# One weight block for two batches, a one-instruction gate and a new order of the start in an attention and feed-forward kernel

## The chip, the cores and the metric

The kernel runs on one core of one Trainium2 chip. The metric is the device time of one execution in microseconds (us), the median of several runs on the same chip. The core has TensorE for matmuls (PE in the profile, PEld for its weight loads), VectorE (DVE), ScalarE (ACT), GpSimd (POOL) and SyncE (SP), which here only issues DMAs. Each engine takes its instructions in the order in which they stand in its own queue and waits at an instruction until what it needs is there.

## The reference

Packed attention and two feed-forward networks follow each other. Eight batches of eight heads have 576 tokens with head size 64; 32 packed queries `p` stand between the two attention steps.

```python
p_packed = sm_attn(p, k, v)              # 32 x 64 for each batch and head
out = sm_attn(q, p_packed, p_packed)     # 576 x 64
x = out.transpose(0, 2, 1, 3).reshape(4608, 512)
h = x @ w_in                             # 512 x 2048
x = (h * (1 / (1 + exp(-1.702 * h)))) @ w_out        # 2048 x 512
h = maximum(maximum(x @ w1, x @ w2), x @ w3)         # 512 x 768 each
return h @ w_out2                        # 768 x 512
```

All is float32. `sm_attn` is the softmax attention with scale 1/8.

## The kernel before

**Splitting.** A float32 product is made of three matmuls of a narrower float32 form: each operand is split into a high and a low part (`hi` by a cast on ACT, `lo` by a subtraction on DVE), and `mm3` (L98 to L102) adds low x high, high x low and high x high. So each product shows as three lines, L100, L101 and L102.

**Attention and the first network in one.** A group is one batch and four heads (`Group`, two groups to a batch). Its steps are: load `p` and `k`, scores `s1` (L237), softmax `sm1`, transposes `t1` and `t1r`, product with `v` (`pv`), transpose `pt` to the packed keys; then the scores `s2` of the queries, softmax `sm2` and `sm3`, and a transpose `tr2` to `at`, with its own hi/lo split. The first network does not use the attention's output: since the packed values are only 32 rows per head, `w_in` is multiplied by them first. That product is called `pw`: 128 rows (four heads x 32) by 512 columns of `w_in` for each batch, group and column block n of four. `h = pw x at` then has the depth of the packed rows.

**Two ways to make `pw`.** For batches 0 and 1, `pw1_unit` (L400) works for one batch and one group: the packed values of two pairs of heads stand in a tile `pt` that holds zeros beside them, so that each of two row blocks c of `w_in` takes one `mm3` with 128 columns of which half are zeros; 6 matmuls of 512 columns. For batches 2 to 7, `pw_unit` (L383) works for a pair of batches: a tile `sp` has the packed values of both batches side by side in its 128 columns, 3 matmuls give 64 rows for each of the two batches, and each half is moved out by its own cast on ACT and subtraction on DVE (64x512, L128 and L129). For batches 2 to 7 `w_in` comes back from `wsc`, a copy of the split weights in DRAM.

**Units.** The first network is cut into 256 units of a batch, half of the tokens (288) and 128 columns of `w_in` (`h_unit`, `g_unit`, `out_unit`, L451 to L500). A unit has 6 matmuls into a bank `h`, the gate, and 12 matmuls into the four banks `acc`; the matmuls of unit n are followed by the output matmuls of unit n-2. The gate is x·sigmoid(1.702x), made as 0.5·x·(1 + tanh(0.851x)): a tanh on ACT (L460), a multiplication on DVE (L461), a cast on ACT (L466) and a subtraction on DVE (L468; on POOL for the first two units). The factor 0.5 is put in when the banks `acc` are moved out (L488 to L494). Two banks `h` exist, so unit n+2 waits until the gate of unit n has read its bank.

**Weights.** The eight weight blocks of `w_in` and the eight of `w_out` arrive as 64-bit patterns and are turned into float32 hi/lo on DVE and ACT (`convert`, `convert_low`: L153 to L187). The first four (`wi0`, `wo0`, `wi1`, `wo2`) are loaded and converted beside the first attention groups.

**Second network.** Its weights are converted late in the first network (`Piece`, `conv_late`, L516 to L579, with sums for a product scheme with fewer matmuls), stored, and loaded back in sets; `Set` (L668) and `out2` (L745) do six blocks of 768 tokens. An output tile `o` has three buffers (L754).

**Order.** Nothing runs in the order of the source. `main` (L804) puts each step into a list with a planned time (tables `D_`, `K_`, `L_`, `Q_`, `R_`, `TP_` and numbers in `main`), sorts it, and issues it; a scheduler in the framework then orders each engine's instructions, so a planned time is a wish. `keep_busy` issues matmuls without use between the first attention groups. Eight PSUM banks are in use: two `ph` (for `h`), two `pa` (for scores, transposes and `pw`), and `c0` to `c3` (for `acc`).

## Time and profile before

| What | Value |
|---|---|
| Median of 3 runs (lowest to highest) | 1327.65 us (1327.56 to 1327.84) |
| The profiled execution: its own time | 1326.56 us |
| Its span (first to last instruction) | 1324.70 us, so 1.86 us lie around it |
| Granted TensorE clock | 1.0 of full speed |
| PE busy | 1302.2 us, 98% |
| DVE busy | 914.6 us, 69% |
| ACT busy | 533.5 us, 40% |
| POOL busy | 118.2 us, 9% |
| Matmuls with a moving operand of 512 columns for `pw` | 96 for batches 0 and 1, 144 for batches 2 to 7 |

The stages, by the first matmul of each: the attention of batches 0 and 1 alone until the first unit at 39.5 us, first output matmul at 50.1 us, units until 780.3 us, second network from 780.4 us to the end. A matmul's busy time in the profile overlaps with the next one's, since matmuls are pipelined: the time that one costs is the distance between two starts. PE at 98% is therefore not a measure of its speed; its idle time is what counts, and the idle time is almost all in the first 60 us.

### The profile page before, as it was taken

The numbers are of one execution on the slowest core, as the hardware profiler recorded it, in microseconds if no ns is written. First come the engines' busy times: TensorE is split into PE (matmuls) and PEld (weight loads), VectorE is DVE, ScalarE is ACT, GpSimd is POOL, SyncE is SP. The second block draws the span as 40 slices with busy tenths as digits, with TensorE's granted clock in tenths as the row PEclk, the third lists the DMA queues.
The fourth block names the chain that finished last, engine by engine and source line by source line (L and its number), as shares of the span: only waits on it lengthen the run. The fifth ranks groups of instructions, "written<-read, shape, count | busy, mean of one in ns | idle before, by whom it ended". The sixth has DMA issues, their size and how long they took to land.

```text
span 1324.7 us, 22337 instructions
## 1 busy us (share of the span) xinstructions
PE 1302.2 (98%) x8614; PEld 1224.6 (92%) x8614; DVE 914.6 (69%) x1864; ACT 533.5 (40%) x1140; POOL 118.2 (9%) x250
## 2 busy tenths in 40 slices
PE   6899999999999999999999999999999999999998
PEld 4699888999999989999999999999899899999997
DVE  7999967864656565679999889636556467366461
ACT  4656544653445444556666532311312213123111
POOL 2300001100000000000000011001011011010000
PEclk9999999999999999999999999999999999999999
DMA  9798635624322330336565659847557476475551
GB/s 348 276 385 317 202 107 163 191 86 137 121 68 85 101 125 31 98 111 220 188 210 168 204 186 358 291 158 272 200 202 251 155 268 236 171 251 199 174 176 48
DMA packets 88874, 249.70 MB, mean 188 GB/s; under 512 B 10176, under 2 KB 39360, under 8 KB 81856
## 3 DMA queue, kind: packets, MB, share of 16 engines
q0 software_dynamic: 24640, 132.66, 29.3%
q1 hardware_dynamic: 64128, 115.62, 25.6%
q8 instruction: 68, 1.11, 0.4%
q14 instruction: 38, 0.31, 0.1%
HBM read 204.47 MB, written 43.78 MB: 187 GB/s over the span
## 4 chain that ended last, share of the span: by engine, by line
PE 93%; DVE 4%; DMA 1%; issue 1%; POOL 0%; ACT 0%; SPq 0%; POOLq 0%; ACTq 0%; DVEq 0%
PE acc L100 10%; PE p L102 10%; PE p L100 10%; PE p L101 10%; PE acc L101 10%; PE acc L102 10%; PE h L100 5%; PE h L102 5%; PE h L101 5%; PE accb L102 4%; PE accb L101 4%; PE accb L100 4%; PE pw L100 1%; PE pw L101 1%; PE pw L102 1%; PE pv L287 1%
## 5 line engine op out<-in xcount | busy, mean ns | idle before, releaser
L100 PE MATMUL acc<-g,wo 128*128 128x288 f32 x1024 | 303.7, 299 | 0.0
L102 PE MATMUL acc<-g,wo 128*128 128x288 f32 x1024 | 300.7, 294 | 0.0
L101 PE MATMUL acc<-g,wo 128*128 128x288 f32 x1024 | 300.1, 294 | 0.6 <-POOL g L468 0.5
L100 PEld LDWEIGHTS acc<-g,wo 128*128 128x128 f32 x1024 | 191.7, 188 | 10.4 <-issue 5.3
L101 PEld LDWEIGHTS acc<-g,wo 128*128 128x128 f32 x1024 | 192.5, 188 | 4.7 <-issue 1.0
L102 PEld LDWEIGHTS acc<-g,wo 128*128 128x128 f32 x1024 | 192.3, 188 | 1.6 <-issue 1.5
L460 ACT ACTIVATE t<-h 128x288 f32<-128x288 f32 x256 | 104.9, 411 | 178.5 <-PE h L102 176.6
L461 DVE SCALAR_TENSOR_TENSOR t<-t,h 128x288 f32<-128x288 f32 x256 | 114.7, 450 | 84.1 <-ACT t L460 82.7
L100 PE MATMUL h<-at,pw 128*128 128x288 f32 x512 | 154.9, 303 | 1.4 <-DVE t L461 1.2
L101 PE MATMUL h<-at,pw 128*128 128x288 f32 x512 | 151.6, 296 | 0.4 <-POOL at L125 0.4
L102 PE MATMUL h<-at,pw 128*128 128x288 f32 x512 | 151.1, 295 | 0.0
L466 ACT CAST g<-t 128x288 fp32r<-128x288 f32 x256 | 110.6, 433 | 94.1 <-DVE t L461 92.9
L468 DVE TENSOR_TENSOR g<-t,g 128x288 fp32r<-128x288 f32 x254 | 114.9, 453 | 35.1 <-ACT g L466 34.3
L681 DVE TENSOR_TENSOR u<-s,p 128x384 f32<-128x384 f32 x54 | 29.9, 553 | 119.4 <-PE p L102 119.1
L100 PE MATMUL p<-x_T,ws 128*128 128x384 f32 x324 | 108.3, 334 | 0.0
L101 PE MATMUL p<-x_T,ws 128*128 128x384 f32 x324 | 108.3, 334 | 0.0
L102 PE MATMUL p<-x_T,ws 128*128 128x384 f32 x324 | 108.2, 334 | 0.0
L100 PEld LDWEIGHTS h<-at,pw 128*128 128x128 f32 x512 | 96.1, 188 | 9.8 <-issue 5.6
L101 PEld LDWEIGHTS h<-at,pw 128*128 128x128 f32 x512 | 96.4, 188 | 1.8 <-POOL at L125 1.3
L102 PEld LDWEIGHTS h<-at,pw 128*128 128x128 f32 x512 | 96.2, 188 | 0.1
L711 ACT COPY s<-p 128x384 f32<-128x384 f32 x54 | 25.9, 479 | 161.9 <-PE p L102 161.7
L129 DVE TENSOR_TENSOR pw<-pw,pw 64x512 fp32r<-64x512 f32 (+1 forms) x110 | 74.9, 686 | 18.6 <-ACT pw L128 17.6
(175 smaller groups left out, 2632.0 us busy)
## 6 DMA issues: line engine op xcount, KB each, us to landing
ws<-wss POOLq DMA_DIRECT2D x54, 1024.0 KB, 7.5
wa<-wsa POOLq DMA_DIRECT2D x54, 768.0 KB, 4.6
wi<-wsc POOLq DMA_DIRECT2D x48, 512.0 KB, 3.9
k<-in_k SPq DMA_DIRECT2D x16, 576.0 KB, 4.5
q<-in_q SPq DMA_DIRECT2D x16, 576.0 KB, 4.3
x2d<-x SPq DMA_DIRECT2D x16, 576.0 KB, 4.0
wss<-ws SPq DMA_DIRECT2D x36, 256.0 KB, 4.0
xr<-x2d SPq DMA_DIRECT2D x24, 384.0 KB, 4.3
```

What stands on the lines that cost most here:

```text
L100: nc.tensor.matmul(o, al, bh, start=start, stop=False, skip_group_check=more)
L101: nc.tensor.matmul(o, ah, bl, start=False, stop=False, skip_group_check=more)
L102: nc.tensor.matmul(o, ah, bh, start=False, stop=stop, skip_group_check=more)
L129: nc.vector.tensor_tensor(out=lo, in0=o, in1=f(hi), op=ALU.subtract)
L287: self.mm = nc.tensor.matmul(o[x * D:x * D + D, :P], self.et[:, c * P + x * D:c * P + x * D + D], self.v[:, c, y * P:y * P + P], start=c = ...
L460: nc.scalar.activation(t, o, AF.Tanh, scale=0.5 * 1.702)
L461: nc.vector.scalar_tensor_tensor(out=t, in0=t, scalar=1.0, in1=o, op0=ALU.add, op1=ALU.mult)
L466: latest["act"] = nc.scalar.copy(g[:, 0], gt[n])
L468: latest["dve"] = eng.tensor_tensor(out=g[:, 1], in0=gt[n], in1=f(g[:, 0]), op=ALU.subtract)
L681: latest["dve"] = nc.vector.tensor_tensor(out=o, in0=a, in1=b, op=op)
L711: latest["act"] = nc.scalar.copy(self.s1, self.b1)
```

## The change

Five things are done, all inside the first network and the start, but for the buffers at the end.

- **Pairs.** For column blocks 1 to 3 of batches 0 and 1, `pw_unit` with pair 0 takes the place of four `pw1_unit` calls each. For that each packed tile `pt` of batches 0 and 1 is also copied into a pair tile `sp`, four POOL copies of 128x64 per group (new L344), which stand in POOL's queue among the copies for the next groups. Block 0 stays as it was.
- **Gate.** Units 8 to 28, 114 to 131 and 189 to 255 (106 units) use one ACT instruction for x·sigmoid(1.702x) instead of tanh and a DVE multiplication; their low part is a plain subtraction. The other 150 units keep tanh and multiplication, and now multiply by 0.5 in the cast and in the subtraction; moving out `acc` no longer multiplies, and for batches 0 and 1 all four `acc` banks are moved out by ACT where a running sum does not exist yet (before: two by ACT, two by DVE). The low parts of units 0 and 1 move from POOL to DVE. The one-instruction gate is in another activation table than the exponential; the built program has 7 more table loads on ACT: at units 8, 114, 116 and 189 for the gate, and ahead of the exponentials of group (2,0), of batch 5 group 1 between units 115 and 116, and of batch 6 group 0 after unit 134.
- **Banks.** The first three groups take their first scores from the banks `ph` and their `pv` and `ptp` from `c0`, which no unit uses yet, instead of from the two `pa` banks.
- **Buffers.** The late weights have 3 raw buffers instead of 2; in the second network a temporary `t` has 3 instead of 4 and the output tile `o` has 2 instead of 3.
- **Plan.** All planned times are new. `k` of group (0,1) is now loaded after `v` and `q` of group (0,0), after `wo0` and after `wi1`; before it was loaded right after `wi0`.

```diff
-D_ = [-2, -8, 2.9, -2.51, 2.83, -0.47, -3.58, -0.6, 0.92, -0.32, -6.66, 0.91, 2.97, 2.32, -5.59, -0.32]
+D_ = [[-4.99, -8, 5.53, ...], [2.8, -9.03, 4.99, ...]]
...
+G_ = [8, 29, 114, 132, 189]
+PAIR0 = 1
...
-    def pa_tile(name):
+    def pa_tile(name, early=None):
+        if early in ("h0", "h1"):
+            return ps_h.tile([P, TB], F32, tag="ph", name=name)
+        if early:
+            return ps_c.tile([P, TB], F32, tag=early, name=name)
         return ps_a.tile([P, TB], F32, tag="pa", name=name)
...
+    EARLY = {"s1_0": "h0", "s1_1": "h1", "pv": "c0", "ptp": "c0"}
...
+            if self.b < 2 and PAIR0 < 4:
+                for x in range(2):
+                    for c in range(2):
+                        d = (c ^ self.b) * P + c * D
+                        nc.gpsimd.tensor_copy(sps[key][x][:, d:d + D], f(to[x][:, c * 192:c * 192 + D]))
...
+    def direct(n):
+        return G_[0] <= n < G_[1] or G_[2] <= n < G_[3] or n >= G_[4]
...
-        nc.scalar.activation(t, o, AF.Tanh, scale=0.5 * 1.702)
-        nc.vector.scalar_tensor_tensor(out=t, in0=t, scalar=1.0, in1=o, op0=ALU.add, op1=ALU.mult)
+        if direct(n):
+            latest["act"] = nc.scalar.activation(t, o, AF.Gelu_apprx_sigmoid)
+        else:
+            nc.scalar.activation(t, o, AF.Tanh, scale=0.5 * 1.702)
+            nc.vector.scalar_tensor_tensor(out=t, in0=t, scalar=1.0, in1=o, op0=ALU.add, op1=ALU.mult)
...
-            elif dc % 2 == 0:
-                nc.scalar.mul(x2[:, dc], o, 0.5)
+            elif dc % 2 == 0 or b < 2:
+                nc.scalar.copy(x2[:, dc], o)
...
-            self.raw = late["r"].tile([P, 2 * TB], I32, tag="raw", bufs=2, name=f"wraw_{self.n}")
+            self.raw = late["r"].tile([P, 2 * TB], I32, tag="raw", bufs=3, name=f"wraw_{self.n}")
...
-            t = late["f"].tile([P, DM], F32, tag="o", bufs=3, name=f"o_{j}_{tt}")
+            t = late["f"].tile([P, DM], F32, tag="o", bufs=2, name=f"o_{j}_{tt}")
...
-                for b in range(2):
-                    add(max(t + .1, tn[start[b, n]] - PL_[b], tpt[b, g]), pw1_unit, b, g, n)
+                for x in range(2):
+                    if n < PAIR0:
+                        add(max(t + .1, tn[start[x, n]] - PL_[x], tpt[x, g]), pw1_unit, x, g, n)
+                    else:
+                        add(max(t + .1, tn[start[0, n]] - 10 + 2 * x, tpt[1, g]), pw_unit, 0, 2 * g + x, n)
```

On PE, at column block 3 of batch 0, the kernel before has these twelve matmuls (`wi0_3` and `wi1_3` are the block's weights for groups 0 and 1, `pt_0_0` the packed tile of batch 0, group 0):

```order
L100 MATMUL pw_0_0_3_1809<-wi0_3_1584,pt_0_0_339 128x512
L101 MATMUL pw_0_0_3_1809<-wi0_3_1584,pt_0_0_339 128x512
L102 MATMUL pw_0_0_3_1809<-wi0_3_1584,pt_0_0_339 128x512
L100 MATMUL pw_0_0_3_1809<-wi0_3_1584,pt_0_0_339 128x512
L101 MATMUL pw_0_0_3_1809<-wi0_3_1584,pt_0_0_339 128x512
L102 MATMUL pw_0_0_3_1809<-wi0_3_1584,pt_0_0_339 128x512
L100 MATMUL pw_0_1_3_1818<-wi1_3_1513,pt_0_1_405 128x512
L101 MATMUL pw_0_1_3_1818<-wi1_3_1513,pt_0_1_405 128x512
L102 MATMUL pw_0_1_3_1818<-wi1_3_1513,pt_0_1_405 128x512
L100 MATMUL pw_0_1_3_1818<-wi1_3_1513,pt_0_1_405 128x512
L101 MATMUL pw_0_1_3_1818<-wi1_3_1513,pt_0_1_405 128x512
L102 MATMUL pw_0_1_3_1818<-wi1_3_1513,pt_0_1_405 128x512
```

In the changed kernel the same place on PE has these six, with the pair tiles `sp` (its lines L114 to L116 are `mm3`):

```order
L114 MATMUL pw_0_0_3_1816<-wi0_3_1518,sp_0_263 128x512
L115 MATMUL pw_0_0_3_1816<-wi0_3_1518,sp_0_263 128x512
L116 MATMUL pw_0_0_3_1816<-wi0_3_1518,sp_0_263 128x512
L114 MATMUL pw_0_2_3_1824<-wi1_3_1430,sp_1_426 128x512
L115 MATMUL pw_0_2_3_1824<-wi1_3_1430,sp_1_426 128x512
L116 MATMUL pw_0_2_3_1824<-wi1_3_1430,sp_1_426 128x512
```

Six more, for the other two row blocks, follow 22 rows later, and with them the block is done for both batches; before, twelve more stand some 300 rows later for batch 1. In each of blocks 1 to 3, 24 matmuls become 12.

On DVE, the end of the softmax of group (0,1) stands before like this, from the maximum's subtraction `a` to the transpose into `at_0_1` (`tmp_wo2`, `raw_wo2` and `wo2` are a weight block's conversion, `pn_1_0` and `pt_1_0` belong to the next batch):

```order
L346 TENSOR_REDUCE st2_0_1_482<-a_0_1_476 128x18
L178 SCALAR_TENSOR_TENSOR tmp_wo2_519<-raw_wo2_249,tmp_wo2_519 128x1024
L180 SCALAR_TENSOR_TENSOR tmp_wo2_519<-raw_wo2_249,tmp_wo2_519 128x1024
L347 TENSOR_SCALAR st2_0_1_482<-st2_0_1_482 128x18
L184 TENSOR_SCALAR raw_wo2_249<-tmp_wo2_519 128x1024
L348 RECIPROCAL st2_0_1_482<-st2_0_1_482 128x18
L185 SCALAR_TENSOR_TENSOR wo2_520<-tmp_wo2_519,raw_wo2_249 128x2x512
L292 SCALAR_TENSOR_TENSOR pn_1_0_540<-pv_1_0_529,st1_1_0_427,mask_87 128x128
L349 TENSOR_TENSOR a_0_1_476<-a_0_1_476,st2_0_1_482 128x576
L129 TENSOR_TENSOR pt_1_0_559<-ptp_1_0_556,pt_1_0_559 128x2x64
L356 STREAM_TRANSPOSE at_0_1_580<-a_0_1_476 128x576
```

In the changed kernel it is this on DVE (its L382 is the transpose, L198 and L199 are the old L184 and L185, L143 is L129):

```order
L194 SCALAR_TENSOR_TENSOR tmp_wo2_590<-raw_wo2_355,tmp_wo2_590 128x1024
L374 RECIPROCAL st2_0_1_492<-st2_0_1_492 128x18
L192 SCALAR_TENSOR_TENSOR tmp_wo2_590<-raw_wo2_355,tmp_wo2_590 128x1024
L375 TENSOR_TENSOR a_0_1_486<-a_0_1_486,st2_0_1_492 128x576
L309 SCALAR_TENSOR_TENSOR pn_1_0_540<-pv_1_0_529,st1_1_0_447,mask_87 128x128
L382 STREAM_TRANSPOSE at_0_1_584<-a_0_1_486 128x576
L198 TENSOR_SCALAR raw_wo2_355<-tmp_wo2_590 128x1024
L143 TENSOR_TENSOR pt_1_0_555<-ptp_1_0_552,pt_1_0_555 128x2x64
L199 SCALAR_TENSOR_TENSOR wo2_591<-tmp_wo2_590,raw_wo2_355 128x2x512
```

The last two conversion steps of `wo2` and the low part of `pt_1_0` now stand behind the transpose into `at_0_1` instead of ahead of it.

## Rows read from the trace of the kernel before

**Rows 1.** Five stretches: us, then busy us of PE, PEld, DVE, ACT, POOL
```profile
core 0: us, PE busy (x) PEld busy (x) DVE busy (x) ACT busy (x) POOL busy (x), PEclk, DMA share, GB/s
5.00:35.00 30.00, 18.74 (x221) 13.46 (x222) 26.12 (x49) 12.88 (x28) 6.78 (x16) 1.00 1.03 383
60.00:200.00 140.00, 139.60 (x1006) 128.17 (x1005) 121.06 (x237) 79.60 (x163) 9.45 (x20) 1.00 0.69 256
80.00:160.00 80.00, 79.89 (x569) 73.81 (x568) 73.94 (x142) 48.29 (x92) 4.51 (x11) 1.00 0.80 298
600.00:760.00 160.00, 158.59 (x1172) 156.01 (x1171) 153.12 (x370) 93.68 (x208) 2.66 (x5) 1.00 0.59 195
760.00:1324.70 564.70, 561.13 (x3071) 535.06 (x3069) 334.49 (x616) 135.13 (x245) 56.16 (x106) 1.00 0.61 211
```

**Rows 2.** Chain that ended last, 30 to 80 us: start us, us, what
```profile
44.38 0.70 DVE at L356
...
45.91 1.40 POOL at L125
50.01 0.81 POOL g L468
...
74.58 2.39 DVE wi L163
```

**Rows 3.** Timeline of PE from 178 us: start us, us, instruction
```profile
178.02 0.40 PE L100 MATMUL pw<-wi,pt 128*128 128x512 f32 x1
...
180.59 0.40 PE L102 MATMUL pw<-wi,pt 128*128 128x512 f32 x1
180.82 0.30 PE L100 MATMUL acc<-g,wo 128*128 128x288 f32 x1
```

**Rows 4.** Groups by line and shape: busy us, mean ns, idle us before
```profile
L461 DVE SCALAR_TENSOR_TENSOR t<-t,h 128x288 f32<-128x288 f32 x256 | 114.7, 450 | 84.1 <-ACT t L460 82.7
L460 ACT ACTIVATE t<-h 128x288 f32<-128x288 f32 x256 | 104.9, 411 | 178.5 <-PE h L102 176.6 <-ACT e L259 0.3 <-ACT g L466 0.2
L129 DVE TENSOR_TENSOR pw<-pw,pw 64x512 fp32r<-64x512 f32 x96 | 65.6, 686 | 17.5 <-ACT pw L128 16.7
L494 DVE TENSOR_SCALAR x<-acc 128x288 f32<-128x288 f32 x32 | 13.6, 449 | 0.0
L220 POOL COPY pbd<-praw 64x64 f32<-64x64 f32 x32 | 10.4, 324 | 17.5 <-DMA praw<-in_p 16.1
L129 DVE TENSOR_TENSOR pw<-pw,pw 128x512 fp32r<-128x512 f32 x14 | 9.2, 683 | 1.0 <-ACT pw L128 0.9
L112 ACT ACT_TABLE_LOAD x1 | 1.3, 1283 | 0.7 <-PEq L996 0.7
```

**Rows 5.** Timeline of DVE, 40 to 45 us
```profile
40.99 0.69 DVE L184 TENSOR_SCALAR raw_wo<-tmp_wo 128x1024 int32<-128x1024 int32 x1
...
41.77 1.17 DVE L185 SCALAR_TENSOR_TENSOR wo<-tmp_wo,raw_wo 128x1024 fp32r<-128x1024 f32 x1
...
44.09 0.29 DVE L129 TENSOR_TENSOR pt<-ptp,pt 128x128 fp32r<-128x128 f32 x1 [0.22 <-ACT pt L128]
44.30 0.77 DVE L356 STREAM_TRANSPOSE at<-a 128x576 f32<-128x576 f32 x1
```

**Rows 6.** Timeline of PE, 13 us: the first scores of group (0,1)
```profile
13.18 1.19 PE L242 MATMUL s<-k,pbd 128*64 128x288 f32 x8 [2.74 <-POOL pbd L220]
```

**Rows 7.** Waits: who waited for whom, us in total, times, longest
```profile
PE h L100 <- DVE t L461: 1.2, 2, 0.9
```

**Rows 8.** Timeline of ACT, second network: first and third of three output tiles
```profile
855.88 0.59 ACT L755 COPY o<-accb 128x512 f32<-128x512 f32 x1 [0.74 <-PE accb L102]
...
858.60 0.59 ACT L755 COPY o<-accb 128x512 f32<-128x512 f32 x1 [0.77 <-PE accb L102]
```

**Rows 9.** DMA issues: times, KB each, median us to landing
```profile
out<-o SPq DMA_DIRECT2D x36, 256.0 KB, 2.0
```

More of the change, by code (lines that the diff above doesn't have):

```diff
@@ L31 @@
 SCALE = 1.0 / D ** 0.5
-D_ = [-2, -8, 2.9, -2.51, 2.83, -0.47, -3.58, -0.6, 0.92, -0.32, -6.66, 0.91, 2.97, 2.32, -5.59, -0.32]
-W_ = [60, 15.02, 42.09, 0]
-K_ = [2, 11, -8, 6, 1, -7, 10, 6, -11, -14, -9, -5, -2, -13, -1, 4]
-L_ = [8.18, 16.49, 4, 22.39]
+W_ = [64.48, 18.42, 56.79, 0]
+K_ = [2.01, 11, -10.89, 8.67, 7.12, -5.04, 5.65, 6.8, -16.14, -14.99, -7.49, 1.03, -5.37, -19.64, 5.48, 3.47]
+L_ = [9.04, 16.23, 0.89, 19.91]
 Z_ = [1, 1, 1, 0, 0, 0, 0, 0, 0, 0, 0, 0, 0, 0, 0, 0]
-PL_ = [10, 12]
-Q_ = [12, 9, 9, 8]
-R_ = [32, 23, 17, 5]
-TP_ = [6.0, 8.5, 5.0]
+PL_ = [10.25, 12.07]
+Q_ = [10, 4, 12, 5]
+R_ = [31, 25, 19, 13]
+TP_ = [6.97, 9.09, 5.28]
+D_ = [[-4.99, -8, 5.53, 5.12, 10.41, -1.7, -4.78, -0.6, -1.23, -3.15, -14.11, -6.79, 3.67, 4.23, 0.62, 2.56], [2.8, -9.03, 4.99, -1.86, -6.98, -0.47, -3.58, -0.31, -6.65, -0.14, -0.97, -0.25, 2.63, 0.24, -9.41, -1.18]]
+A_ = [-1.26, 8.77, 21.07, 33.84]
+AS_ = [0.78, 1.07, 0.91, 0.94]
+T_ = [40.71, 1.23, 1.16, 10]
+B2_ = [70.77, 18, 1.2, 5.18]
+B4_ = [20, 10.7, 1.2, 38]
+PC_ = [-11.47, 6.42, 5.47, 8.52, 9, 15.08, 10.31, 11.78]
+G_ = [8, 29, 114, 132, 189]
+X_ = [252, 2.6]
+PAIR0 = 1
 @with_exitstack
@@ L207, in __init__ @@
             self.swap = b & 1 if b >= 2 else 0
+            self.early = EARLY if 2 * b + g < 3 else {}
         def load_pk(self):
@@ L304, in pt @@
                 to = ptt[self.b, self.g] = [t[:, HALF * x:HALF * x + 2 * P] for x in range(2)]
+                key = 0, self.g
+                if key not in sps and PAIR0 < 4:
+                    t = u_tile(f"sp_{self.g}", F32R)
+                    sps[key] = [t[:, HALF * x:HALF * x + 2 * P] for x in range(2)]
             else:
@@ L465, in g_unit @@
         g = gp.tile([P, 2, HALF], F32R, tag="g", name=f"g_{n}")
-        latest["act"] = nc.scalar.copy(g[:, 0], gt[n])
-        eng = nc.gpsimd if n < 2 else nc.vector
-        latest["dve"] = eng.tensor_tensor(out=g[:, 1], in0=gt[n], in1=f(g[:, 0]), op=ALU.subtract)
+        if direct(n):
+            latest["act"] = nc.scalar.copy(g[:, 0], gt[n])
+            latest["dve"] = nc.vector.tensor_tensor(out=g[:, 1], in0=gt[n], in1=f(g[:, 0]), op=ALU.subtract)
+        else:
+            latest["act"] = nc.scalar.mul(g[:, 0], gt[n], 0.5)
+            latest["dve"] = nc.vector.scalar_tensor_tensor(
+                out=g[:, 1], in0=gt[n], scalar=0.5, in1=f(g[:, 0]), op0=ALU.mult, op1=ALU.subtract
+            )
         gt[n] = g
@@ L580, in load_wo2 @@
     def load_wo2(fc):
-        raw = late["r"].tile([P, 2 * TB], I32, tag="raw", bufs=2, name=f"wraw_o{fc}")
+        raw = late["r"].tile([P, 2 * TB], I32, tag="raw", bufs=3, name=f"wraw_o{fc}")
         nc.sync.dma_start(raw, w_out2[fc])
@@ L797, in attention @@
             after = {9: 7, 13: 12, 12: 11, 11: 10, 10: 8, 8: 6, 6: 5, 5: 3, 3: 1, 4: 2, 1: 0}.get(k)
-            tk = t + dt * stretch + (D_[k] if b == 0 else 0) + (dq if k in (7, 9, 11, 12, 13) else 0)
+            tk = t + dt * stretch + (D_[g][k] if b == 0 else 0) + (dq if k in (7, 9, 11, 12, 13) else 0)
             ts.append(tk if after is None else max(tk, ts[after] + .05))
```

43 lines of the change are left out of this document (21 added, 22 removed).

## The prediction

> **What bounds the kernel now.** I read the stretches first [rows 1]. From 60 us to the end PE is idle for 0.4 us of 140, 1.4 of the 160 late ones and 3.6 of the last 565, while DVE is busy 86% from 60 to 200 us and 96% from 600 to 760. So after 60 us whatever is taken off PE shortens the kernel, as long as DVE can follow. The reader is to see there that the two numbers belong to different questions: PE sets the pace, DVE is the engine that would set it next. The first 60 us are another stage: the chain of waits [rows 2] runs through DVE until the transpose that makes `at` of group (0,1), then ACT and POOL split it, and only then can the first unit be finished; its gate's low part on POOL (0.81 us) is the last thing before output matmuls flow. The chain comes back to DVE at 74.58 us, where a conversion of `w_in` is waited for. So the start is a DVE queue, and what stands in it ahead of that transpose counts.
>
> **The change part by part.**
>
> *Pairs.* A batch's block was 2 groups of 6 matmuls, so 24 for the two batches, and is 12 now, since one 128-column operand carries both batches without zeros. Three blocks: 36 matmuls fewer. Twelve of them stand on PE between 178.02 and 180.82 us [rows 3], that is 0.233 us from start to start (the 0.40 us of a row overlaps the next). 36 x 0.233 = 8.4 us. They stood after 60 us, beside other PE work, and all of PE's work there is on the path: -8.4 us.
>
> The price is on DVE: a block's eight results are moved out as halves of 64 partitions, which take as long as whole ones (686 against 683 ns [rows 4]). Three blocks had 12 subtractions and have 24: 12 x 0.686 = +8.2 us. Taken away in the same stretch are the gate multiplications of 21 units (8 to 28), 21 x 0.450 = 9.5 us, and 8 moves of `acc` that ACT now does, 8 x 0.449 = 3.6 us. Together DVE loses 4.8 of 121.1 us in the stretch in which PE loses 8.4 of 140. Its share would go from 86% to 88%. Tightest is 80 to 160 us, where DVE was busy 73.9 of 80 us [rows 1] and most of the new subtractions fall: there PE loses only about 3 us and DVE may gain one. I take +0.5 us of new PE waits; bounds -0.4 (what PE lost there before) and +4.
>
> *Start.* The old L184, L185 and L129 no longer stand ahead of the transpose for (0,1): from start to next start 0.6, 1.1 and 0.2 us [rows 5], 1.9 us off the DVE chain. What is late next is POOL: in its queue two copies into the pair tile for the next batch now stand ahead of the low part of `at`; the nearest row is a POOL copy of 64x64 at 324 ns [rows 4], the new ones are 128x64; 2 x 0.32 = 0.6 us if they are not hidden by the wait for ACT. The low part of the first unit's gate moves from POOL to DVE, where a maximum, a subtraction and two reductions of other groups stand between; I count that at nothing. Sum -1.3, say -1.4 with a little for the waits that vanish. Bounds: DVE was idle 3.9 of the 30 us from 5 to 35 [rows 1], so at best 1.9 + 3.9 = -5.8; at worst all eight new copies for the first two groups delay it, 2.6 - 1.9 = +0.7.
>
> *Early banks.* They only lift waits for `pa`; the units need `ph` and `c0` after 39 us, when these uses are over. Nothing by itself; its worth is inside the start.
>
> *Gate.* Of 1.2 us that PE waited for the multiplication at two units [rows 7], both after 600 us, and 1.4 us that it was idle there in all, the units from 189 on remove the cause: 67 x 0.450 = 30 of DVE's 153 us in that stretch. I take -1.3; bounds 0 and -1.4. The new instruction is not in the trace; the tanh takes 411 ns for the same bank [rows 4]. Were it twice that, the gate would still be shorter than tanh plus multiplication, 861 ns. The other 150 units have the same number of instructions; multiplying in the cast and subtraction is free by shape.
>
> *Table loads.* Seven, each 1283 ns [rows 4], 9.0 us of ACT. ACT waits 176.6 us for `h` over the 256 units, 0.69 us for each, and a load needs no operand, so it runs in that wait and is late by about 0.6 us; the unit after the next, which needs the bank, then has the multiplication's 0.45 us in hand and twelve output matmuls besides. I take +0.5 in all; bounds 0 and 9.0.
> The Trainium skill, "ScalarE: Activation LUTs", says in its section "Rules for kernel authors" to budget about 2.7 us for every switch to a different set. The row above shows 1.28 for the load and an ACTIVATE right after it, so the trace does not bear out more for the load itself; by the page the seven would be 18.9 us of ACT, an estimate that only matters if none of it is hidden.
>
> *Buffers.* With two `o` tiles the third copy in a row, 2.7 us after the first [rows 8], waits for the first's store, which lands 2.0 us after its issue in the median [rows 9]; issue follows the copy (0.6 us), so it is late by nothing at the median. Behind it on ACT stand only further output copies, and PE needs that bank one round of output tiles later. 0 for this, and 0 for `t`, which only DVE writes and reads. The third raw buffer lets loads run ahead: 0.
>
> Sum: -8.4 - 1.4 - 1.3 + 0.5 + 0.5 = -10.1 us. Against the profiled execution's own 1326.56 us that is 1316.5; the median of the runs shown is 1.1 us above it, so 1317.5 us.
>
> **Rivals.**
>
> 1. *DVE takes over from 80 to 160 us.* For it: 92% busy, halves that cost as much as wholes, conversions in the same queue. Against it: half of the removed matmuls or more stood later, where DVE has room. Half of PE's gain given back, +4.2: 1321.7 us.
>
> 2. *The start gets later.* `k` of group (0,1) now stands behind 3.3 MB more (`v`, `q`, `wo0`, `wi1`) at 383 GB/s [rows 1], an estimate of 8.6 us; the scores started at 13.18 us, and POOL was what they waited for [rows 6]. For it: DVE's chain for (0,1) begins with them. Against: DVE has a weight conversion and the softmax of (0,0) to do meanwhile. If half of the delay shows, +4.3 in place of -1.4: 1323.2 us.
>
> 3. *Table switches stop PE; slower.* If the load does not run ahead but in the gate's line, each costs PE the load and the restart of one gate, 1.28 + 0.41 + 0.45 = 2.1 us; seven are 15.0 in place of 0.5: 1332.0 us. It decides from 1.5 us each, where the rest of the gain is used up; the trace's ACT, idle half of the time, speaks against it. The skill's rule quoted above would have it so, with 18.9 us.
>
> 4. *The new order also removes what PE still loses.* All idle time after 60 us up to 760 gone (2.8 us) and the best start: 1317.5 - 4.4 - 2.5 = about 1310.6 us.
>
> **How the numbers follow.** Forecast 0.66, rival 1 0.13, rival 2 0.08, rival 3 0.05, rival 4 0.08. A run of this kernel can tell about 0.2% (2.7 us) from no change: faster means below 1325.0, slower above 1330.3. Forecast, rivals 1 and 4 and nearly all of 2 are faster: 0.91. Rival 3 at its full price is slower, 0.04; what lies between is 0.05. The range: low end at rival 4, 1310.5; high end just above rival 2, 1324.0. Forecast alone: 1314 to 1321.
>
> **What would show it.** Right: 36 fewer 512-column matmuls for `pw`; PE still idle under 1 us from 60 to 200; the first output matmul about 1.4 us earlier than 50.1; the second network's first matmul about 10 us earlier than 780.4; its length unchanged. Wrong: PE rows from 80 to 160 that wait for DVE or for a conversion (rival 1); scores of (0,1) that wait for `k`, and a first output matmul after 50.1 (rival 2); PE waits just behind a table load, or a gate instruction well over 0.86 us (rival 3); a second network that is longer than before (a buffer after all).

## The result, and the profile after

The changed kernel takes 1315.38 us in the median of four runs (1313.53 to 1315.88); the kernel before took 1327.74 us in four runs beside it. The ratio is 0.9901, with a 95% interval from 0.9884 to 0.9918. The forecast was 1317.5 us, range 1310.5 to 1324.0. The profiled execution took 1315.11 us, its span is 1313.0 us (before 1324.7): 11.7 us less.

To see where they went, the span is cut at events that both kernels have: the first output matmul, and the first matmul of units 16, 48 and 184 in the timeline of PE. The 18 matmuls of a unit are the same in both, so a stretch is shorter by the matmuls that left it or by waits that ended. Times in us:

| Stretch | before | changed | difference |
|---|---|---|---|
| start to first output matmul | 50.1 | 50.9 | +0.8 |
| to unit 16 | 43.5 | 44.1 | +0.6 |
| units 16 to 48 (60 matmuls of `pw`, then 24) | 104.4 | 97.2 | -7.2 |
| units 48 to 184 (123 of `pw` in both) | 399.6 | 397.3 | -2.3 |
| unit 184 to the end | 727.1 | 723.5 | -3.6 |
| span | 1324.7 | 1313.0 | -11.7 |

The second network alone took 544.2 us in both. All 36 matmuls left units 16 to 48; 36 x 0.233 = 8.4 us were taken out and 1.2 of them came back. PE's idle time shows only 0.25 us of that: it was 0.11 us in this stretch before and is 0.36 now.

The stretches of [rows 1], read in the changed kernel:

```profile
core 0: us, PE busy (x) PEld busy (x) DVE busy (x) ACT busy (x) POOL busy (x), PEclk, DMA share, GB/s
5.00:35.00 30.00, 20.39 (x218) 14.34 (x218) 25.38 (x46) 12.62 (x27) 8.43 (x15) 0.89 0.96 349
60.00:200.00 140.00, 138.71 (x1014) 127.30 (x1013) 124.37 (x232) 92.39 (x190) 11.06 (x22) 1.00 0.70 257
80.00:160.00 80.00, 79.64 (x568) 73.52 (x567) 75.93 (x132) 59.70 (x115) 4.51 (x11) 1.00 0.79 297
600.00:760.00 160.00, 160.00 (x1202) 159.17 (x1201) 137.54 (x315) 97.05 (x211) 2.53 (x4) 1.00 0.56 188
```

From 600 to 760 us PE is never idle now (the waits of [rows 7] have no row any more), and VectorE has 137.5 us of work there in place of 153.1. From 80 to 160 us VectorE is fuller than before (75.9 of 80, before 73.9) and PE still hardly waits. The first row has the surprise: a granted clock of 0.89 near the start, where before it was 1.00.

The groups that answer to [rows 4]; the columns are those of before:

```profile
L143 DVE TENSOR_TENSOR pw<-pw,pw 64x512 fp32r<-64x512 f32 x120 | 81.9, 687 | 21.1 <-ACT pw L142 19.5
L490 ACT ACTIVATE t<-h 128x288 f32<-128x288 f32 x106 | 43.5, 411 | 59.9 <-PE h L116 59.1
L490 ACT ACT_TABLE_LOAD x4 | 5.1, 1283 | 2.7 <-PE h L116 2.7
L344 POOL CAST sp<-pt 128x64 fp32r<-128x64 f32 x16 | 10.1, 664 | 1.3 <-ACT pt L142 1.2
```

The one-instruction gate takes 411 ns like the tanh. The third row says that ScalarE's idle time ahead of the four loads (2.7 us) was ended by `h`: these loads did not run while ScalarE waited for `h`; they started when `h` was there and stand between `h` and the gate. On ScalarE, at units 8 and 9:

```profile
76.32 1.28 ACT L490 ACT_TABLE_LOAD   x1 [2.44 <-PE h L116]
77.62 0.71 ACT L490 ACTIVATE t<-h 128x288 f32<-128x288 f32 x2
```

PE has no idle time in the 6 us behind any of the seven added loads all the same. A copy into a pair tile takes 664 ns in the mean; I had priced it at 324.

What stood at the place of [rows 6], PE before the first scores of group (0,1), and POOL in the same time:

```profile
14.37 1.19 PE L351 MATMUL s<-q,ptf 128*64 128x288 f32 x8 [0.35 <-ACT ptf L338]
21.38 2.19 PE L259 MATMUL s<-k,pbd 128*64 128x288 f32 x8 [5.83 <-POOL pbd L237]
...
17.93 0.76 POOL L237 COPY pbd<-praw 64x64 f32<-64x64 f32 x1 [4.31 <-DMA praw<-in_p]
18.63 2.40 POOL L344 CAST sp<-pt 128x64 fp32r<-128x64 f32 x2
21.10 0.23 POOL L237 COPY pbd<-praw 64x64 f32<-64x64 f32 x1
```

The scores came 8.2 us later than before. `praw` landed at 17.8 us (before 11.7), and then two pair copies, 2.40 us, stood between the two halves of `pbd`. PE was idle for 5.8 us.

At the end of the start, [rows 2] had the low part of `at` of (0,1) on POOL at 45.91 and the gate's low part on POOL at 50.01. Now, on POOL and then on VectorE:

```profile
45.13 1.48 POOL L344 CAST sp<-pt 128x64 fp32r<-128x64 f32 x2 [1.23 <-ACT pt L142]
46.57 1.39 POOL L139 TENSOR_TENSOR at<-at,at 128x576 fp32r<-128x576 f32 x1
...
49.03 0.46 DVE L493 SCALAR_TENSOR_TENSOR t<-t,h 128x288 f32<-128x288 f32 x1 [1.77 <-ACT t L492]
...
51.46 0.45 DVE L503 SCALAR_TENSOR_TENSOR g<-t,g 128x288 fp32r<-128x288 f32 x1
```

Two more pair copies end just before the low part of `at`, and the gate's low part waits behind four instructions of other groups, left out here. Neither is what made the start late. The low part of `at` ends 2.40 us after ScalarE's cast; in the kernel of "Late copies" below, where no copy stands ahead of it, it takes 2.27 us instead of 1.39 and ends 2.42 us after the cast (before: 1.54). And for the gate's low part PE waits 0.37 us, where it waited 0.45 before.

What is late is the first unit: its first matmul starts at 41.4 us (before 39.5), and from there to the first output matmul it is 9.5 us (before 10.6). PE waits ahead of it for zeros that POOL writes into a tile `pt`:

```profile
38.95 0.50 PE L114 MATMUL pw<-wi,pt 128*128 128x512 f32 x1 [1.80 <-POOL pt L320]
```

```profile
35.70 1.12 POOL L237 COPY pbd<-praw 64x64 f32<-64x64 f32 x2 [3.49 <-DMA praw<-in_p]
36.90 1.74 POOL L139 TENSOR_TENSOR at<-at,at 128x576 fp32r<-128x576 f32 x1
38.60 0.30 POOL L320 MEMSET pt<- 128x256 f32 x1
```

The zeros stand in POOL's queue behind the low part of `at` of (0,0), and that behind a copy of a `praw` that landed at 35.6 us (in the kernel before, the one at this place landed at 32.1).

### The profile page after: what moved, and what is told of

Its sections match the earlier page's. It is cut to its first block, busy times and chain, and to the rows that moved or that the text cites. A ratio compares the mean times of both kernels' runs of the same rounds, so it can differ in the third digit from the quotient of the medians.

```text
span 1313.0 us, 22139 instructions
## 1 busy us (share of the span) xinstructions
PE 1292.8 (98%) x8578; PEld 1219.2 (93%) x8578; DVE 884.3 (67%) x1764; ACT 552.6 (42%) x1167; POOL 128.4 (10%) x264
## 4 chain that ended last, share of the span: by engine, by line
PE 93%; DMA 2%; DVE 2%; POOL 1%; issue 1%; ACT 1%; SPq 0%; POOLq 0%; DVEq 0%; ACTq 0%
PE acc L114 10%; PE p L116 10%; PE p L115 10%; PE p L114 10%; PE acc L115 10%; PE acc L116 10%; PE h L114 5%; PE h L116 5%; PE h L115 5%; PE accb L115 4%; PE accb L116 4%; PE accb L114 4%; PE pv L304 1%; PE s L351 1%; PE s L259 1%; DMA praw<-in_p 1%
## 5 line engine op out<-in xcount | busy, mean ns | idle before, releaser
L114 PE MATMUL acc<-g,wo 128*128 128x288 f32 x1024 | 304.9, 299 | 0.2 <-DVE x L525 0.2
L116 PE MATMUL acc<-g,wo 128*128 128x288 f32 x1024 | 300.6, 294 | 0.0
L114 PEld LDWEIGHTS acc<-g,wo 128*128 128x128 f32 x1024 | 191.8, 188 | 9.2 <-issue 5.1
L116 PEld LDWEIGHTS acc<-g,wo 128*128 128x128 f32 x1024 | 192.3, 188 | 1.0 <-issue 0.9
L114 PE MATMUL h<-at,pw 128*128 128x288 f32 x512 | 154.3, 301 | 0.0
L116 PE MATMUL h<-at,pw 128*128 128x288 f32 x512 | 151.7, 296 | 0.0
L493 DVE SCALAR_TENSOR_TENSOR t<-t,h 128x288 f32<-128x288 f32 x150 | 67.5, 451 | 74.2 <-ACT t L492 73.5
L492 ACT ACTIVATE t<-h 128x288 f32<-128x288 f32 x150 | 61.7, 411 | 122.4 <-PE h L116 121.3
L114 PE MATMUL p<-x_T,ws 128*128 128x384 f32 x324 | 108.3, 334 | 0.0
L116 PE MATMUL p<-x_T,ws 128*128 128x384 f32 x324 | 108.1, 334 | 0.0
L114 PEld LDWEIGHTS h<-at,pw 128*128 128x128 f32 x512 | 96.3, 188 | 7.8 <-issue 6.5
L143 DVE TENSOR_TENSOR pw<-pw,pw 64x512 fp32r<-64x512 f32 (+1 forms) x122 | 83.2, 686 | 21.1 <-ACT pw L142 19.5
L116 PEld LDWEIGHTS h<-at,pw 128*128 128x128 f32 x512 | 96.2, 188 | 1.3 <-issue 1.3
L502 ACT ACTIVATE g<-t 128x288 fp32r<-128x288 f32 x150 | 66.7, 446 | 50.0 <-DVE t L493 49.5
L503 DVE SCALAR_TENSOR_TENSOR g<-t,g 128x288 fp32r<-128x288 f32 x150 | 69.1, 461 | 25.5 <-ACT g L502 25.0
```

What stands on the lines that cost most here:

```text
L114: nc.tensor.matmul(o, al, bh, start=start, stop=False, skip_group_check=more)
L116: nc.tensor.matmul(o, ah, bh, start=False, stop=stop, skip_group_check=more)
L143: nc.vector.tensor_tensor(out=lo, in0=o, in1=f(hi), op=ALU.subtract)
L492: nc.scalar.activation(t, o, AF.Tanh, scale=0.5 * 1.702)
L493: nc.vector.scalar_tensor_tensor(out=t, in0=t, scalar=1.0, in1=o, op0=ALU.add, op1=ALU.mult)
L502: latest["act"] = nc.scalar.mul(g[:, 0], gt[n], 0.5)
```

## The experiments

All stretches are in us, as in the table above; "median" is of all runs of a kernel, the stretches are of the profiled one. The kernel before ran beside each group, on several chips, and took 1326.9 to 1328.2 us in the median, so a difference of about 1 us between kernels of different groups tells nothing.

| Kernel | to first output | to 16 | 16 to 48 | 48 to 184 | 184 to end | median |
|---|---|---|---|---|---|---|
| before | 50.1 | 43.5 | 104.4 | 399.6 | 727.1 | 1327.7 |
| changed | 50.9 | 44.1 | 97.2 | 397.3 | 723.5 | 1315.4 |
| changed, again | 50.7 | 44.0 | 97.2 | 397.3 | 723.3 | 1315.0 |
| no pairs | 48.0 | 43.9 | 103.9 | 397.3 | 723.8 | 1318.7 |
| before with pairs | 50.9 | 44.5 | 110.2 | 398.9 | 726.0 | 1333.9 |
| no gate | 49.9 | 44.0 | 102.9 | 397.3 | 724.3 | 1322.5 |
| all gates | 50.0 | 45.3 | 97.6 | 397.8 | 733.8 | 1326.3 |
| old plan | 53.7 | 44.4 | 102.1 | 398.9 | 727.8 | 1329.6 |
| old buffers | 51.5 | 44.0 | 97.2 | 397.3 | 732.6 | 1323.8 |
| late copies | 49.0 | 44.0 | 97.1 | 397.3 | 723.7 | 1313.6 |
| late copies, again | 47.6 | 44.0 | 97.1 | 397.3 | 724.1 | 1313.2 |
| late copies, POOL gate | 50.8 | 45.0 | 97.1 | 397.3 | 723.6 | 1314.8 |
| late copies, early `k` | 55.1 | 44.0 | 97.1 | 397.3 | 724.3 | 1319.6 |
| late copies, PE filled | 51.4 | 44.0 | 97.1 | 397.3 | 723.6 | 1315.3 |

### No pairs

```diff
-PAIR0 = 1
+PAIR0 = 4
```

> The changed kernel with the old way of blocks 1 to 3 (six matmuls for each batch and group, 36 more of 512 columns in all) and without the 16 copies into the pair tiles; all else, the plan too, stays. Theory (the pairs are worth their matmuls, 36 x 0.233 = 8.4 us, and the copies on GpSimd cost the start about 1 us): 1315.4 + 8.4 - 1 = 1322.8 us, 1321.5 to 1324. First rival (VectorE gave part of it back through the 24 half-size subtractions): less than that returns, 1318 to 1321. Second rival (most of the gain came from the new plan and the gate, the pairs are hidden): under 1318 us.

Measured: 1318.71 us, ratio to before 0.9931 (0.9919 to 0.9944). Only 3.3 us more than the changed kernel: the first rival's range, at its low end. But the stretches give another reason than the rival's. Units 16 to 48 are 6.7 us longer, so little of the 8.4 us was given back there; the first output matmul comes 2.9 us earlier without the pair copies.

### Before with pairs

```diff
+                    if n < 1:
                         add(max(t + .1, ...), pw1_unit, b, g, n)
+                    else:
+                        add(max(t + .1, tn[start[0, n]] - 10 + 2 * b, tpt[1, g]), pw_unit, 0, 2 * g + b, n)
```

with the pair tiles and the four copies of `pt` (L318 to L344 of the changed kernel).

> The kernel before with the pairs alone (pair tiles, their 16 GpSimd copies, 36 matmuls fewer); old gate, plan, banks and buffers. Theory (PE bounds everything after 60 us, the copies cost the start about 1 us): 1327.7 - 8.4 + 1 = 1320.3 us, 1319 to 1321.5. Rival (without the shorter gate in 80 to 160 us VectorE, busy 92% there, has 8.2 us more to do and PE waits for it): 1322 to 1326 us, with PE waits for VectorE between 80 and 200 us.

Measured: 1333.90 us, ratio 1.0048 (1.0035 to 1.0060): slower than before, and slower than either side expected. PE's waits from 95 to 206 us, as "who waited for whom: us in total, times, longest" (the kernel before has no row in that stretch):

```profile
PE ptp L298 <- DVE pn L292: 2.3, 1, 2.3
PE acc L100 <- DVE x L497: 1.5, 2, 1.4
PE pw L100 <- DVE pw L129: 1.5, 1, 1.5
PE h L100 <- DVE t L470: 1.2, 1, 1.2
...
PE acc L101 <- DVE g L477: 0.7, 1, 0.7
```

Most are waits for VectorE. With the longest of them, which ends at 160.97 us, the granted clock also fell to half (PEclk is the third number from the end):

```profile
159.90:166.70 6.80, 5.73 (x19) 3.83 (x20) 3.72 (x10) 1.30 (x4) 0.00 (x0) 0.50 0.21 76
```

It is the same 36 matmuls, and units 16 to 48 are 5.8 us longer than before instead of 8.4 shorter: 14.2 us lost, of which PE's idle time shows 9.0.

### No gate

```diff
-G_ = [8, 29, 114, 132, 189]
+G_ = [999, 999, 999, 999, 999]
```

> The changed kernel with tanh and multiplication in all 256 units: 106 x 0.45 = 48 us more on VectorE, and no table loads but the first. Theory (the short gate takes away PE's waits in acc and h after 200 us, most of them after 600 us): 1.5 to 3 us longer, 1317 to 1318.5 us, with the waits back at 600 to 650 us. First rival (it is what lets VectorE keep up with the pairs at 80 to 160 us): 4 us or more, above 1319.4 us, with waits there. Second rival (the table loads cost about as much as the shorter gate gives): 1314 to 1316 us.

Measured: 1322.47 us, ratio 0.9956 (0.9942 to 0.9969), the first rival. The profiled run was the shortest of the five (1320.5). Units 16 to 48 are 5.7 us longer than in the changed kernel, the stretch after unit 184 only 0.8. PE's longest waits in this kernel from 93 to 197 us, then the only one of the changed kernel from 95 to 192 us:

```profile
PE h L114 <- DVE t L493: 1.4, 1, 1.4
PE pw L114 <- DVE pw L143: 1.0, 1, 1.0
PE acc L114 <- DVE x L525: 0.9, 2, 0.6
...
```

```profile
PE acc L114 <- DVE x L525: 0.2, 1, 0.2
```

The 106 gate units were mostly worth it at the 21 units beside the pairs, not at the 67 late ones.

### Old plan

All 14 tables of planned times hold the values of before, two of them shown; pairs, gate, banks and buffers stay:

```diff
-A_ = [-1.26, 8.77, 21.07, 33.84]
+A_ = [0.0, 8, 20, 34]
...
-PC_ = [-11.47, 6.42, 5.47, 8.52, 9, 15.08, 10.31, 11.78]
+PC_ = [-8, 4, 5, 6.5, 9, 0, 10, 10.5]
```

> The changed kernel (pairs, gate, banks, buffers) with all planned times as before. The pairs alone made the old kernel 6 us slower, and without the gate the changed kernel is 7 us slower. Theory (pairs need both: the gate takes work from VectorE, and the new plan spreads what is left): the gate repairs about half of the loss, 1324 to 1329 us, with PE waits for VectorE left between 95 and 205 us. Rival (the gate alone makes room for the pairs, the plan only orders the start): 1315 to 1319 us. A time above 1331 would mean that the gate's place, units 8 to 28, does not meet the waits of the old plan.

Measured: 1329.60 us, ratio 1.0010 (1.0000 to 1.0020). All of the gain is gone, a little beyond the theory's range. It goes in every stretch: 2.8 us at the start, 4.9 in units 16 to 48, 1.6 in 48 to 184, 4.3 after.

With these four kernels, the stretch of units 16 to 48 can be set side by side. Without waits, 104.4 - 8.4 = 96.0 us would be left:

| | old plan | new plan |
|---|---|---|
| pairs, tanh only | 110.2 (14.2 lost) | 102.9 (6.9 lost) |
| pairs, short gate | 102.1 (6.1 lost) | 97.2 (1.2 lost) |
| no pairs | 104.4 (tanh) | 103.9 (short gate) |

The gate gives 8.1 us with the old plan and 5.7 with the new one, the plan 7.3 or 4.9. (The left column's tanh kernel also has the old banks and buffers, and moves `acc` out on both engines.) PE's idle time in the stretch is 9.0, 4.2, 3.4 and 0.4 us in the four kernels with pairs, in the order of the table's rows, and the granted clock in it 0.97, 1.00, 0.98 and 1.00, so with the old plan a part of the loss is slow matmuls behind the waits. The plan's part is one of order and not of work: with the old plan VectorE is busy for 86.4 us of the stretch, in the changed kernel for 87.7, without the gate for 93.5.

### All gates

```diff
-G_ = [8, 29, 114, 132, 189]
+G_ = [0, 999, 999, 999, 999]
```

> The changed kernel with the one-instruction gate in all 256 units, so between the exponentials too: 50 table loads on ScalarE in place of 8, 42 more, 150 x 0.45 = 68 us less on VectorE. Theory (a load runs while ScalarE would wait for h, and PE does not see it): loads cost PE under 0.1 us each, VectorE's relief gives back up to 3 us of the waits that PE has at 95 to 192 us: 1312 to 1318 us. Rival (each switch stands in the gate's line and costs PE 2.1 us, as worked out in the third rival of the prediction): 42 x 2.1 = 88 us, 1403 us; at 1.28 us each, the load alone, 1369 us. In between, the excess over 1315.4 divided by 42 is the price of a switch.

Measured: 1326.29 us, ratio 0.9988 (0.9979 to 0.9997). That is 10.9 us above the changed kernel, far from 88. All 42 added loads stand before 582 us, and from the first output to unit 184 it took 540.7 us in place of 538.6: 2.1 / 42 = 0.05 us per load, with VectorE's relief already set against it. So PE hardly sees them, and the third rival falls by its price. Its condition, the load in the gate's line, holds: all 25 loads ahead of a gate start after the last `h` matmul of their unit. What hides them must then be the room behind the gate, until unit n+2 needs the bank; that was not tested by itself. The Trainium skill, "ScalarE: Activation LUTs", section "Rules for kernel authors", budgets about 2.7 us per switch, by which 42 would be an estimated 113 us; the run does not bear that out for PE.

Most of the loss stands where no load is, 10.3 us after unit 184, 7.8 of them in the second network. On VectorE and PE early in the second network, and the granted clock behind it:

```profile
787.31 0.55 DVE L716 TENSOR_TENSOR m<-u,p 128x384 f32<-128x384 f32 x1 [6.40 <-DMA wss<-ws]
...
790.06 0.69 PE L114 MATMUL p<-x_T,wa 128*128 128x384 f32 x1 [4.88 <-DVE u L716]
```

```profile
788.90:795.70 6.80, 5.64 (x18) 5.65 (x19) 6.49 (x17) 1.34 (x2) 1.17 (x2) 0.50 0.40 146
```

VectorE waited 6.4 us at a store of a late weight, PE 4.9 us behind it, and then the clock was at half for 6.8 us. Why the order at this place came out differently was not followed further, so the cause of these 10 us stays open.

### Old buffers

```diff
-            self.raw = late["r"].tile([P, 2 * TB], I32, tag="raw", bufs=3, ...)
+            self.raw = late["r"].tile([P, 2 * TB], I32, tag="raw", bufs=2, ...)
... (and in load_wo2)
-                t = f_tile("t", 3, f"t_{self.n}_{c}")
+                t = f_tile("t", 4, f"t_{self.n}_{c}")
...
-            t = late["f"].tile([P, DM], F32, tag="o", bufs=2, ...)
+            t = late["f"].tile([P, DM], F32, tag="o", bufs=3, ...)
```

> The changed kernel with the buffers of before: 2 raw buffers for the late weights, 4 of t and 3 of the output tile. Theory (the prediction's zero for all three; what PE no longer loses after 590 us comes from the plan and the gate): 1315.4 us within 1 us. Rival (the third raw buffer removes about 2 us of waits in acc between 590 and 680 us): 1317 to 1318 us, with PE's waits back in that stretch.

Measured: 1323.79 us, ratio 0.9962 (0.9948 to 0.9975): 8.4 us more, where I expected none and the rival 2. Nearly all of it lies in one place: from unit 240 to the second network it takes 49.2 us in place of 41.1. The chain that ended last, in the kernel with the old buffers (start us, us, what):

```profile
731.20 0.44 DVE wraw_o L562
...
732.98 0.60 SPq L581
733.62 11.08 DMA wraw<-in_w
```

then on VectorE and on PE:

```profile
744.82 0.43 DVE L554 TENSOR_SCALAR c<-wraw 128x512 int32<-128x512 int32 x1 [5.68 <-DMA wraw<-in_w]
```

```profile
746.36 0.40 PE L114 MATMUL h<-at,pw 128*128 128x288 f32 x1 [2.70 <-ACT t L490]
...
749.40 0.58 PE L114 MATMUL acc<-g,wo 128*128 128x288 f32 x1 [1.99 <-DVE x L525]
749.78 0.44 PE L115 MATMUL acc<-g,wo 128*128 128x288 f32 x1
750.02 0.44 PE L116 MATMUL acc<-g,wo 128*128 128x288 f32 x1
```

With two raw buffers the load of a late piece must wait until a block of `w_out2` is converted and its buffer is free. It is issued from 732.4 us on, behind four loads of `x` (730.05), and has landed at 744.7. The conversion stands at a fixed place in VectorE's queue, where VectorE waits 5.68 us for it, and blocks the gates behind it. In the changed kernel the same load is issued ahead of those of `x`, at 721.5 us, and has landed at 726.8:

```profile
721.53 0.55 SPq L579 DMA_DIRECT2D wraw<-in_w  x1
722.14 1.07 SPq L581 DMA_DIRECT2D wraw<-in_w  x2
723.30 1.91 SPq L657 DMA_DIRECT2D xr<-x2d  x4
```

The last PE rows are 0.24 us from start to start where 0.13 is usual: the granted clock is 0.5 from 748.5 to 755.3 us. The buffers of the second network, `t` and `o`, aren't in use at that time, and the second network takes 544.2 us here too, so the raw buffer is the one that counts; it was not undone by itself.

### Late copies

The 16 copies into the pair tiles stand in a step `sp` of their own, planned so that they come behind the low part of `at` of (1,0):

```diff
-                        nc.gpsimd.tensor_copy(sps[key][x][:, d:d + D], f(to[x][:, ...]))
+        if b < 2 and PAIR0 < 4:
+            add(SP_[2 * b + g], grp.sp)
```

> The changed kernel with the 16 copies into the pair tiles moved behind the low part of at of (1,0) in GpSimd's queue, all at about 60 us; nothing else is changed. Theory (these copies, two of them 2.4 us ahead of the second half of pbd of (0,1) and two of them 1.5 us ahead of the low part of at of (0,1), are what made the start later, and PE's idle time before those scores is what brought the granted clock down): scores of (0,1) at about 19 us in place of 21.4, the granted clock higher between 18 and 25 us, low part of at about 1 us earlier, first output matmul about 1 us earlier, 1314.3 us. Rival (the start hangs on praw and k of (0,1), which land 6 and 10 us later than before, and on VectorE's queue): scores earlier, but the first output matmul and the time unchanged, 1315.4 within 0.5 us.

Measured: 1313.60 us (1312.83 to 1317.62), ratio 0.9898 (0.9883 to 0.9912), first output matmul at 49.0. The clock did not stay up (0.61 from 18 to 25 us). Since the difference to the changed kernel is below what one comparison can tell, it ran once more:

> The kernel with the pair copies at about 60 us once more; its five runs before spread from 1312.8 to 1317.6 us, and the changed kernel's eight from 1313.5 to 1315.9. Theory (the copies cost the start 1 to 2 us): 1313 to 1314 us, first output matmul at 49.0 us. Rival (the earlier difference was the spread of the start, which hangs on when praw of (0,1) lands): 1314.5 to 1316 us.

Measured: 1313.21 us (1312.08 to 1317.74), ratio 0.9901 (0.9885 to 0.9918), first output matmul at 47.6. For comparison the changed kernel itself ran a second time, without an edit:

> The changed kernel itself once more, beside the next two, so that differences of 1 to 2 us can be read from runs of one chip: 1315.4 us within 1 us, first output matmul at 50.9 us.

Measured: 1314.98 us (1313.46 to 1315.71), ratio 0.9906 (0.9892 to 0.9919), first output matmul at 50.7.

(The first late copies had four runs before this, not five.) The nine runs with late copies have a median of 1313.25 us, the eight of the changed kernel one of 1315.2. This is the best version of the study, but 2.0 us, 0.15%, is less than is surely told apart.

The first output matmul was at 49.9 to 51.5 us in the five profiles with the new plan and early copies (changed twice, old buffers, no gate, all gates) and at 47.6 to 49.0 in three without (late copies twice, no pairs). Counted from the first exponential on ScalarE, which itself starts anywhere from 7.5 to 9.3 us, it comes after 41.1 to 43.4 us with early copies and after 39.8, 39.8 and 40.5 without. So the start is shorter without them, by 0.6 to 3.6 us. But the three tries below also have the copies late, and there it is 43.0, 43.6 and 47.1 us: the order of other steps weighs as much, and the copies' own part is not shown. The wait of 1.80 us for the zeros of `pt` stands in two of the five (the first profile of the changed kernel and old buffers), in none of the three, and again in the first try.

### Three tries at the start

A halving and the subtraction for the first unit's gate on POOL (`u` is a tile for the halved value; its line is left out):

```diff
+            if n < 1:
+                nc.gpsimd.tensor_scalar(out=u, in0=gt[n], scalar1=0.5, scalar2=None, op0=ALU.mult)
+                nc.gpsimd.tensor_tensor(out=g[:, 1], in0=u, in1=f(g[:, 0]), op=ALU.subtract)
```

> The kernel with the pair copies moved to about 60 us (1313.6 us), and the low part of the first unit's gate on GpSimd again (a halving beside ScalarE's cast, then the subtraction) in place of VectorE, where two reductions, a maximum and a subtraction stand ahead of it. Theory (the first output matmuls wait for that low part): the second output matmul about 0.8 us earlier, 1312.8 us. Rival (VectorE's queue decides the units after it anyway, so the lead is lost by unit 8): 1313.6 within 0.5 us.

Measured: 1314.78 us, ratio 0.9899 (0.9885 to 0.9914); first output at 50.8, unit 16 another 1 us later. No gain: the start was later before the first gate already, since PE waited 1.80 us for the zeros of `pt` at 37.88 us, behind a `praw` that landed at 34.6 (32.1 and 33.4 in the two profiles of late copies). Nor is the low part sooner: on POOL it ends at 53.35 us, 2.6 us behind the first output matmul, on VectorE in the changed kernel at 51.91, 1.0 us behind it.

`p` and `k` of (0,1) loaded early:

```diff
-D_ = [[-4.99, ...], [2.8, -9.03, ...]]
+D_ = [[-4.99, ...], [-6.5, -9.03, ...]]
```

> The kernel with the pair copies at about 60 us, and p and k of group (0,1) loaded right behind the first weight block again, ahead of v and q of (0,0). Its scores waited 3.3 us for k there. Theory (second rival of the prediction: the late k costs start time, hidden so far behind VectorE): scores of (0,1) at 13 to 15 us in place of 20.4, no half clock before them, first output matmul 1 to 3 us earlier than 49.0, 1311 to 1312.6 us. Rival (VectorE's queue sets the start; earlier scores only put q of (0,0) and wo0 later): first output matmul at 49 us or later, 1313 to 1316 us.

Measured: 1319.63 us, ratio 0.9943 (0.9931 to 0.9956). The scores started at 12.5 us, and yet the first output matmul is 6.1 and 7.5 us later than in the two profiles with the late `k`. On VectorE the two maxima of these scores (L268) stand among the steps of `wo0`, and PE's transposes behind them waited:

```profile
22.05 0.78 DVE L192 TENSOR_SCALAR tmp_wo<-raw_wo 128x1024 int32<-128x1024 int32 x1
22.75 0.44 DVE L268 TENSOR_REDUCE st<-s 128x1 f32<-128x288 f32 x1
23.11 1.21 DVE L193 SCALAR_TENSOR_TENSOR tmp_wo<-raw_wo,tmp_wo 128x1024 f32<-128x1024 uint16 x1
24.25 1.25 DVE L195 SCALAR_TENSOR_TENSOR tmp_wo<-raw_wo,tmp_wo 128x1024 int32<-128x1024 int32 x1
25.42 0.44 DVE L268 TENSOR_REDUCE st<-s 128x1 f32<-128x288 f32 x1
...
27.27 1.17 PE L291 MATMUL t<-ident,e 128*128 128x128 f32 x4 [8.02 <-ACT e L277]
```

50 matmuls without use in PE's gap before the scores of (0,1), issued behind the second scores of (0,0) (three lines that place them are left out):

```diff
-    BUSY = {(0, 0): (44, 6, 12, 0), ...}
+    BUSY = {(0, 0): (44, 6, 12, 0, 50), ...}
...
-... lambda: (self.s2(0), self.s2(1), self.sm2()) ...
+... lambda: (self.s2(0), self.s2(1), self.busy(4), self.sm2()) ...
```

> The kernel with the pair copies at about 60 us, and 50 more matmuls without use (2.8 us) on PE between the second scores of (0,0) and the first of (0,1), where PE waits 3.3 us for k and where the granted clock then is 0.5 for 6.8 us. Theory A (the idle time brings the clock down, and the slow matmuls behind it delay the start): granted clock 1.0 there, the scores of (0,1) 1.2 in place of 2.2 us long, first output matmul 0.5 to 1 us earlier, 1312.8 us. Theory B (the clock stays up but the start hangs on VectorE): clock 1.0, first output matmul at 49.0 within 0.3 us, 1313.6 us. Rival: the clock falls all the same.

Measured: 1315.26 us (1312.23 to 1317.22), ratio 0.9908 (0.9895 to 0.9922). The clock was 1.0 at the scores, which took 1.19 us in place of 2.19, but fell to 0.5 from 24.9 to 31.7 us, behind a next wait of 2.5 us. First output at 51.4. So neither theory nor rival holds as stated: the low clock was only moved, and what it costs the start stays open.

## Why the prediction came out right

The total was right, in part by luck: the start and the pairs came out 2.2 and 1.3 us worse than forecast, the late units and those from 48 to 184 came out 2.3 and 2.8 us better, and these cancel in good part. By its own steps, in us of the span:

| Step | forecast | measured |
|---|---|---|
| pairs, and VectorE's answer (to unit 48 from the first output) | -8.4 + 0.5 | -6.6 |
| start | -1.4 | +0.8 |
| gate after 600 us (unit 184 to the end) | -1.3 | -3.6 |
| table loads; units 48 to 184, otherwise not priced | +0.5 | -2.3 |
| buffers, early banks | 0 | in the above |
| sum | -10.1 | -11.7 |

- **Pairs.** The price from start to start was right: 36 matmuls left, and 1.2 us of 8.4 came back in units 16 to 48. The reason for the small return was argued as a balance of busy time on VectorE (8.2 us in, 13.1 out). The runs bear out half of it: without the gate, which is work, 6.9 us come back. But with the old plan, which is order alone, it is 6.1, and without both 14.2. VectorE's busy time from the first output to unit 48 fell by 0.6 us (129.4 to 128.8), not by the 4.8 of the balance; the new plan also moves other steps into this stretch. The first rival, VectorE as the bound, did not come in the whole change (1.2 us against its 4.2); where the cover is taken away it is enough to make the pairs a loss. What I missed is that the new plan covers nearly as much as the gate.
- **Start: the term that failed.** It had -1.4 us, and +0.8 was measured. VectorE's chain did get shorter: the transpose for (0,1) moved from 44.30 to 43.83, and from the first unit to the first output it takes 1.1 us less. The two copies ahead of the low part of `at` of (0,1), priced at 0.6 us, cost nothing there, as the low part ends 2.4 us after the cast with and without them; and the gate's low part was rightly counted at nothing. What the term left out is POOL's queue further ahead: the first unit starts 1.9 us later, with PE waiting 1.80 us for zeros behind a late `praw`. The other two copies, which hold the scores of (0,1), are a part of that at most; the kernels with late copies start sooner (47.6 and 49.0; the forecast's -1.4 would be 48.7), but the tries show that this is not theirs alone.
- **The second rival** described what happened: `k` landed at 19.4 us in place of 9.8 and the scores started 8.2 us later. Only 1.9 us of that reach the first unit, so most of it was hidden, as argued. What the late `k` costs by itself is not shown, for the try with an early `k` also put other steps in another order and made the start worse.
- **Gate.** Its late part is worth 0.8 us, not 1.3, and its main worth is beside the pairs. The other 2.8 us of the last stretch go with the plan and the third raw buffer: without the one or without the other, that stretch is longer than before (727.8 and 732.6). Of the 2.3 us between units 48 and 184, 1.6 go with the plan: the two kernels with the old one have 398.9 there, and all with the new one 397.3 to 397.8; 0.7 is gone in the old kernel with pairs already, and why is open. The fourth rival said so, for 2.8 us.
- **What idle time hides.** The term's bound of -1.4 and the fourth rival's 2.8 us were read from PE's idle time. In the two stretches it was 1.0 and 1.4 us before and is 0 now, and yet 5.9 us are gone. A wait takes more than its idle time, since the modelled end of the matmul ahead covers its beginning. In the kernel before:

```profile
608.63 0.29 PE L100 MATMUL acc<-g,wo 128*128 128x288 f32 x1
609.09 0.40 PE L101 MATMUL acc<-g,wo 128*128 128x288 f32 x1 [0.17 <-DVE g L468]
```

  The two starts are 0.46 us apart where 0.13 is usual, so 0.33 us are lost and 0.17 listed.
- **Table loads.** 0.05 us each, net, where 0.07 was forecast, but not by the reason given: a load was to run in the wait for `h`, and it runs behind `h`, in the gate's line. (The row in [rows 4] shows the load's length alone; that the gate follows at once is seen in the changed kernel.)
- **Buffers.** Zero was right for the tiles of the second network as far as its unchanged length shows. For the raw buffer "lets loads run ahead: 0" was wrong: without it the new plan loses 8.4 us. Whether it would help the old plan was not tried.
- **What would show it.** 36 matmuls fewer, the second network's length and its earlier begin (11.6 us, forecast 10) were seen. The first output matmul was not earlier, and after 50.1, which was the second rival's sign. PE's idle time from 60 to 200 us is 1.3 us, above the 1 us named; 0.9 of it are two waits ahead of unit 16, for VectorE at 62.9 and for POOL at 75.7.

## What to carry to other kernels

Taking each part out one by one costs 3.3 (pairs), 7.1 (gate), 8.4 (buffers) and 14.2 us (plan), 33 us in all, where the whole change gives 12.4. When PE is the bound and a second engine is nearly so, an edit that takes work off PE and puts it on the other must be priced together with what makes room there; alone it can be a loss of 6 us. Ask of every new small instruction, and of every load that is moved, what stands behind it in its queue at each of its places, not at the one place that you are looking at. And take PE's idle time as the least that its waits cost.
